# Limits through one partition, a list of places for all pieces of work, and bit operations placed one by one, in a fused attention and feed-forward kernel

## The chip, the cores and the metric

The kernel runs on one core of one Trainium2 chip. Its engines work side by side, each through its own queue in order: TensorE (PE, with its weight loads as PEld), VectorE (DVE), ScalarE (ACT), GpSimd (POOL) and SyncE (SP), which here issues nearly all DMA transfers. The metric is the device time of one execution in microseconds (us); less is better.

## The reference

Sliding-window attention with a few global keys, then a feed-forward layer with a piecewise-quadratic activation. Four batches, 8 heads, 768 positions, head size 64; the feed-forward layer sees 3072 rows of 512, with an inner width of 2048.

```python
def _attn_ref(q, k, v, n_global, n_local):
    scores = (1.0 / np.sqrt(D)) * np.matmul(q, k.transpose(0, 1, 3, 2))
    rel = pos[:, None] - pos[None, :]
    is_global = pos[None, :] < int(n_global)
    is_local = (rel >= 0) & (rel < int(n_local))
    keep = is_global | is_local
    dist = np.where(is_global & ~is_local, float(n_local), np.abs(rel))
    bias = -slopes[:, None, None] * dist[None, :, :]
    scores = np.where(keep, scores + bias[None], -1e9)
    a = softmax(scores)
    return np.matmul(a, v)

def _moe_ref(x, w_in, w_out):
    h = x @ w_in
    g = np.where(h >= 1, h, np.where(h <= -1, 0.0, (h + 1) ** 2 / 4.0))
    return g @ w_out
```

`n_global` (8) and `n_local` (96) are inputs, 64-bit integers in device memory. `w_in` and `w_out` come as 64-bit floats, so the kernel has to make 32-bit floats of them from their two halves with bit operations.

## The kernel before

**Tiles.** A unit is a block of 128 query rows of one batch; there are 24. The first four units are the first blocks of the four batches; they see one block of keys and run in 32-bit floats (`first_*`). The other 20 see their own block, the one before it and the global keys; they run with each operand split in two 16-bit halves (`put_unit` and what it calls). A unit is handled in two halves of four heads (`hf`). Two units make a chunk of 256 rows for the feed-forward layer; there are 12 chunks.

**Feed-forward.** `ffn1(c, g)` is 24 matmuls of 256 columns (2 blocks of 128 inner columns, 4 blocks of the depth, three products of halves) into one PSUM tile; `gelu(c, g, s)` follows in five steps (s = 0 on ScalarE, 1 and 2 on VectorE, 3 on ScalarE, 4 on GpSimd); `ffn2(c, t, f)` is three matmuls of 512 columns that add inner block `f` into the output of row tile `t`. `ffn2(c, t, f)` needs weight piece 16 + f, `ffn1(c, g)` the pieces 2g and 2g + 1.

**Weights.** Each of the 32 pieces (16 of `w_in`, then 16 of `w_out`) is loaded as 512 KB of raw words into one of three buffers (`w_load`, line 279, SP's queue), put together by three VectorE operations over 128 x 512 (`w_bits`, lines 293, 295 and 298, one after the other, the middle result in a PSUM tile of a pool with one buffer), rounded to the high half (`w_hi`, ScalarE), scaled in place (`w_scale`, line 306: two pieces of three on ScalarE, the third on GpSimd, by `WENG`), and subtracted to the low half (`w_lo`, GpSimd).

**The limits.** The two integers are fetched to all 128 partitions (line 103, ScalarE's DMA queue), made one float each in four small VectorE operations (lines 107 to 114), and used in `distances` (lines 245 to 247) to build the table of distances, which `slope` scales to a bias for each head. `masked` (line 373) adds the bias and takes the row's limit, `expo` is the exponential. `positions` (line 215) makes a row of column numbers by doubling, the partition numbers by a small matmul (line 225), and the unit matrix. `warm` (line 261) issues matmuls of zeros.

**Keys and values.** `fetch` loads a block into a ring of six buffers (shared by first loads and fetches), `conv_hi` and `conv_lo` make the halves, `conv_check` squares the block for a later check. `keep_glob` keeps the global keys of a batch and `set_glob` copies them into the block before the unit's own (keys by GpSimd, line 528, by `KGE`; values by VectorE, line 530). `scores`, `attend` are the matmuls; `turn_p`, `turn_x` are transposes by DMA.

**What sets the order.** Every call is put in a plan with a planned time (`at`), the plan is sorted by time, and the calls are made in that order; each engine's queue gets its instructions in this order and keeps it. The planned times are constants at the head of the file and are not times of the chip. Waits between engines come from the tiles that are read and written. The weights are read a second time later for a check of their range (`check_load`, `check_reduce`).

Of the kernel before, what the change touches and what calls it, by code (L numbers as in the profile page):

```python
# [17 lines left out]
P = 128  # L18
# [30 lines left out]
WENG = "aap"  # L49
# [6 lines left out]
KGE = "gpsimd"  # L56
# [7 lines left out]
FLOAD = [-2.88, 2.56, 12.5, 19.72]  # L64
VLOAD = [-0.57, 11.85, 18.46, 26.87]
FIRST = [8.37, 11.4, 14.3, 17.89, 30.69, 41.68, 52.21, 58.42]
WARM = [(1.0, 10)]
WLOAD = [0.8, 1.0, 8.0]
WA = 3
T0 = 27.51  # L70
GA = 5.33
GB = 5.56
TAB = -0.77
TBC = -2.29
RC = 42.99
WL = 10.75
E3 = [-19.46, -14.0, -6.46, -0.47, 3.78, 9.72, 16.26, 20.67]
PER = 47.0
SOFF = -14.3
FETCH = 16.6  # L80
CONV = 8.83
KG = 4.08
CHK = 7.36
VCONV = 10.53
VFETCH = 8.51
AVL = 15.92
GEL = [2.7, 3.48, 4.29, 5.77, 6.57]
# [9 lines left out]
def attention_then_moe(ctx, tc, q, k, v, n_global, n_local, w_in, w_out, out):  # L97
# [9 lines left out]
    nf = cpool.tile([P, 2, 2], F32, name="nf")  # L107
    nc.vector.tensor_copy(nf, nraw)
    neg = cpool.tile([P, 2, 2], F32, name="neg")
    nc.vector.tensor_single_scalar(neg, nf, 0.0, op=ALU.is_lt)  # L110
    nlow = cpool.tile([P, 2], F32, name="nlow")
    nc.vector.scalar_tensor_tensor(nlow, neg[:, :, 0], 4294967296.0, nf[:, :, 0], op0=ALU.mult, op1=ALU.add)
    nval = cpool.tile([P, 2], F32, name="nval")
    nc.vector.scalar_tensor_tensor(nval, nf[:, :, 1], 4294967296.0, nlow, op0=ALU.mult, op1=ALU.add)
# [9 lines left out]
    with ExitStack() as fast:  # L124
        fast_path(fast, tc, q, k, v, ng, nl, w_in, w_out, out, half, nm, sums, sq, su)
# [43 lines left out]
def fast_path(ctx, tc, q, k, v, ng, nl, w_in, w_out, out, half, nm, sums, sq, su):  # L169
    nc = tc.nc  # L170

# [36 lines left out]
    zeros = const.tile([P, DM], F16, name="zeros")  # L208
# [5 lines left out]

    def positions():
        nc.vector.memset(zeros, 0.0)
        nc.vector.memset(jrow[:, 0:1], 0.0)
        one = const.tile([P, 1], F32, name="one")
        nc.vector.memset(one, 1.0)
        n = 1  # L220
        while n < WIN:
            nc.vector.tensor_scalar(jrow[:, n : 2 * n], jrow[:, 0:n], float(n), None, op0=ALU.add)
            n *= 2
        pps = ps_h.tile([P, 1], F32, tag="h", name="pps")
        nc.tensor.matmul(pps, jrow[0:1, 0:P], one[0:1, :], start=True, stop=True)
        nc.vector.tensor_copy(prow[:, 0:1], pps)
        nc.vector.tensor_scalar(prow[:, 1:2], pps, float(P), None, op0=ALU.add)
        nc.vector.tensor_scalar(ident, jrow[:, 0:P], prow[:, 0:1], None, op0=ALU.is_equal)

    dists = {}  # L230

    def distances(own):
# [11 lines left out]
        nc.vector.tensor_copy(gap[:, 0:w], jrow[:, 0:w])  # L244
        nc.vector.tensor_scalar(cut, gap, ng, BIG, op0=ALU.is_ge, op1=ALU.mult)
# [13 lines left out]
    fill = []  # L259

    def warm(n):
        if not fill:
            fill.append(ps_o.tile([P, DM], F32, tag="o", name="fill"))
        for _ in range(n):
            nc.tensor.matmul(fill[0], zeros[:, 0:P], zeros, start=True, stop=True)
# [19 lines left out]
    def w_bits(n, s):  # L285
# [3 lines left out]
        if s == 0:  # L289
            wbits[n] = ps_b.tile([P, *hi.shape[1:]], I32, tag="b", name=f"w{num}_bits")  # L290
        t = wbits[n]
        if s == 0:
            nc.vector.tensor_scalar(t, rh, 0x07FFFFFF, 3, op0=ALU.bitwise_and, op1=ALU.logical_shift_left)  # L293
        elif s == 1:
# [5 lines left out]

    def w_hi(n):
        num, src, hi, lo = piece(n)
        nc.scalar.activation(hi, wf[n], AF.Copy, scale=SW)
# [88 lines left out]
    def norm(u, hf, scale):  # L392
        whole(u, hf)
        c = u * H + hf * 4
        r = xp.tile([P, 4], F32, tag="r", name=f"r{u}_{hf}")
        nc.vector.tensor_scalar(r, sums[:, c : c + 4], TINY, scale, op0=ALU.add, op1=ALU.mult)
        nc.vector.reciprocal(r, r)
        rs[u, hf] = r
# [30 lines left out]
    def scale_x(u, hf):  # L429
        x = xp.tile([P, 4, D], F32, tag="x", name=f"x{u}_{hf}")  # L430
# [26 lines left out]
    def put_first(u, hf, s):  # L457
# [5 lines left out]
        at(s + FO[3], norm, u, hf, 1.0 / SV)  # L463
# [150 lines left out]
    def put_unit(u, s0, s1):  # L614
# [26 lines left out]
        for hf, s in ((0, s0), (1, s1)):  # L641
# [8 lines left out]
            at(t + UO[5], norm, u, hf, SP_)  # L650
# [98 lines left out]
    at(0.5, distances, True)  # L749
    for h in range(H):  # L750
# [9 lines left out]
    TB = T0 + 8 * GA + TAB  # L760
    R1 = TB + 8 * GB + TBC
    R2 = R1 + RC
    tw = []
    for g in range(8):
        t = T0 + GA * g
        tw += [t - WL, t - WL + GA / 2]
        put_ffn1(0, g, t)
        if WA:
            at(t + 2.65, warm, WA)
    for g in range(8):  # L770
        t = TB + GB * g
# [12 lines left out]
    for c in range(2, NU // 2):  # L784
# [208 lines left out]
```

## Time and profile before

| what | us |
|---|---|
| median of three runs (lowest, highest) | 649.54 (649.40, 650.46) |
| the profiled execution's own time | 649.53 |
| its span, first to last instruction | 647.7 |
| TensorE busy | 613.5 |
| VectorE busy | 426.8 |
| ScalarE busy | 407.6 |
| GpSimd busy | 288.3 |

The mean granted clock of TensorE is 0.965 over the span. The page of the profile gives each engine's busy time, and 40 slices of the span with the busy share in tenths; its groups are instructions of one line, operation and tile, with count, busy time, mean length, and what ended the idle time before them. A timeline row has start, length, engine, line, operation, what is written and read, and in brackets the idle time ahead of it and its releaser.

### The profile page before, as it was taken

Reading aid. Unit: us, or ns where it says so; the run is one execution under the profiler, and the core shown is the slowest. Engines: PE = TensorE matmul, PEld = TensorE weight load, DVE = VectorE, ACT = ScalarE, POOL = GpSimd, SP = SyncE. Lnnn points to the kernel's source line nnn. Section 1 sums busy time; section 2 is a strip of 40 time slices with the busy share of each in tenths; the row PEclk is TensorE's granted clock in tenths of the full one; section 3 lists DMA queues with packets and bytes.
Section 4 is the critical chain, followed back from the end, with each engine's and each line's share of the span. In section 5 each row is a group of like instructions: output and inputs, shape, how many; then the busy total and the mean of one; then the engine's idle time right before and its main releaser. Section 6 shows DMA issues by size and latency. Waiting matters only on the chain.

```text
span 647.7 us, 14690 instructions
## 1 busy us (share of the span) xinstructions
PE 613.5 (95%) x5588; PEld 420.1 (65%) x5588; DVE 426.8 (66%) x1093; ACT 407.6 (63%) x1060; POOL 288.3 (45%) x292
## 2 busy tenths in 40 slices
PE   5688898899999999999999999999999999999995
PEld 3555665565786766766776676677667667666652
DVE  4699989976686655655767756666766766743351
ACT  2566667898876776666677667657767667532220
POOL 0056466985357345344454444445534534322210
PEclk8678899799999999999999999999999999999998
DMA  5465455729573453254466375394574463431141
GB/s 194 129 197 163 141 160 204 229 67 186 150 156 59 104 135 108 54 149 129 115 164 176 101 191 156 86 196 127 141 202 138 101 195 97 114 124 57 42 161 40
DMA packets 144367, 88.08 MB, mean 136 GB/s; under 512 B 108448, under 2 KB 124832, under 8 KB 144288
## 3 DMA queue, kind: packets, MB, share of 16 engines
q1 hardware_dynamic: 144000, 87.05, 49.4%
q8 instruction: 46, 0.75, 0.5%
q14 instruction: 33, 0.27, 0.1%
q10 hardware_dynamic: 288, 0.00, 0.0%
HBM read 54.53 MB, written 6.29 MB: 94 GB/s over the span
## 4 chain that ended last, share of the span: by engine, by line
PE 79%; DVE 13%; ACT 4%; issue 2%; DMA 1%; POOL 0%; DVEq 0%; ACTq 0%
PE o L715 36%; PE h L672 32%; PE s L545 4%; PE av L588 4%; DVE w_bits L295 2%; DVE w_f L298 2%; DVE w_bits L293 2%; PE av L424 1%; DVE h L690 1%; ACT z L385 1%; DVE u L695 1%; DMA nraw<-in_n_local_dram 1%; DVE z L373 1%; ACT u L685 1%; DVE x L431 1%
## 5 line engine op out<-in xcount | busy, mean ns | idle before, releaser
L672 PE MATMUL h<-xt,wih 128*128 128x256 f16 x1536 | 262.5, 276 | 1.3 <-DVE u L695 0.9
L672 PE MATMUL h<-xt,wil 128*128 128x256 f16 x768 | 212.0, 276 | 0.0
L703 POOL TENSOR_TENSOR gl<-u,gh 128x512 f16<-128x512 f32 x96 | 120.4, 1254 | 192.1 <-ACT gh L699 166.9
L672 PEld LDWEIGHTS <-wih 128*128 128x128 f16 x1536 | 149.7, 99 | 33.1 <-DVE u L695 1.7
L385 ACT ACTIVATE z<-z,nm 128x256 f32<-128x256 f32 (+1 forms) x192 | 92.1, 481 | 93.0 <-DVE nm L373 92.7
L715 PE MATMUL o<-wol,gh 128*128 128x512 f16 x384 | 146.5, 381 | 1.4 <-POOL wol L317 1.4
L715 PE MATMUL o<-woh,gh 128*128 128x512 f16 x384 | 146.8, 382 | 0.3 <-ACT ob L729 0.3
L715 PE MATMUL o<-woh,gl 128*128 128x512 f16 x384 | 146.3, 381 | 0.0
L373 DVE CUSTOM_DVE_ANT_0 z<-s,bias 128x256 f32<-128x256 f32 (+1 forms) x192 | 69.2, 394 | 87.4 <-PE s L545 82.2
L715 PEld LDWEIGHTS <-gh 128*128 128x128 f16 x768 | 71.5, 98 | 68.7 <-issue 1.6
L690 DVE SCALAR_TENSOR_TENSOR h<-h,u 128x512 f32<-128x512 f32 x96 | 66.7, 695 | 71.1 <-ACT u L685 69.9
L699 ACT ACTIVATE gh<-u 128x512 f16<-128x512 f32 x96 | 59.7, 621 | 41.0 <-DVE u L695 40.9
L672 PEld LDWEIGHTS <-wil 128*128 128x128 f16 x768 | 76.0, 99 | 10.1 <-issue 0.5
L685 ACT ACTIVATE u<-h,half 128x512 f32<-128x512 f32 x96 | 64.5, 672 | 25.0 <-PE h L672 24.8
L695 DVE SCALAR_TENSOR_TENSOR u<-u,h 128x512 f32<-128x512 f32 x96 | 65.8, 686 | 4.9
L715 PEld LDWEIGHTS <-gl 128*128 128x128 f16 x384 | 37.7, 98 | 47.7 <-issue 3.0
L563 DVE SCALAR_TENSOR_TENSOR ph<-z,ph 128x1024 f16<-128x1024 f32 x40 | 54.4, 1360 | 15.2 <-ACT ph L561 15.2
L341 DVE TENSOR_REDUCE sq<-c_raw 128x1 f32<-128x256 f32 x128 | 48.7, 410 | 3.9 <-DMA c_raw<-in_moe_w_out_dram 3.9
L500 POOL TENSOR_SCALAR kr<-kr 128x512 f32<-128x512 f32 x24 | 17.2, 717 | 66.0 <-ACT kh L485 65.7
L561 ACT ACTIVATE ph<-z 128x1024 f16<-128x1024 f32 x40 | 42.2, 1056 | 1.1
L545 PEld LDWEIGHTS <-qh 64*128 64x128 f16 x960 | 27.4, 95 | 18.7 <-issue 10.4
L588 PEld LDWEIGHTS <-pt 128*128 128x128 f16 x960 | 33.5, 98 | 8.7
(93 smaller groups left out, 690.1 us busy)
## 6 DMA issues: line engine op xcount, KB each, us to landing
w_raw<-in_moe_w_in_dram SPq DMA_DIRECT2D x16, 512.0 KB, 3.6
w_raw<-in_moe_w_out_dram SPq DMA_DIRECT2D x16, 512.0 KB, 3.5
c_raw<-in_moe_w_in_dram SPq DMA_DIRECT2D x32, 256.0 KB, 3.2
c_raw<-in_moe_w_out_dram SPq DMA_DIRECT2D x32, 256.0 KB, 3.0
kr<-in_k_dram SPq DMA_DIRECT2D x28, 256.0 KB, 4.4
vr<-in_v_dram SPq DMA_DIRECT2D x28, 256.0 KB, 3.2
qr<-in_q_dram SPq DMA_DIRECT2D x24, 256.0 KB, 4.6
out_dram<-ob SPq DMA_DIRECT2D x24, 256.0 KB, 3.3
```

The costliest lines, as they stand in the source:

```text
L373: nc.vector.tensor_tensor_reduce(out=p32[u, hf][:, hh, :], in0=pts[u, hf][hh // 2][:, hh % 2, 0:n], in1=bias[:, 4 * hf + hh, base : base + n],
L385: nc.scalar.activation(z, z, AF.Exp, bias=nm[:, c : c + 1], scale=-1.0, accum_out=sums[:, c : c + 1])
L545: nc.tensor.matmul(pair[r][:, j, e * P : (e + 1) * P], qf[rows, a, 2 * hf + j, :], kf[rows, c, 2 * hf + j, :], start=(n == 0), stop=(n == 2),)
L563: nc.vector.scalar_tensor_tensor(phs[u, hf][:, 1, :], zf, SP_, phs[u, hf][:, 0, :], op0=ALU.mult, op1=ALU.subtract)
L588: nc.tensor.matmul(av[:, hh, :], pt[:, a, hh, kt, :], vt[:, c, h * D : (h + 1) * D], start=(n == 0), stop=(n == 5),)
L672: nc.tensor.matmul(hp[:, e, :], w[:, dc, f], xt[:, hf, 2 * a + j, :], start=(n == 0), stop=(n == 3 * NDC - 1),)
L685: nc.scalar.activation(us[c, g], hs[c, g], AF.Relu, bias=half, scale=2.0 / (SV * SW), accum_out=su[:, col : col + 1])
L690: nc.vector.scalar_tensor_tensor(ws[c, g], hs[c, g], 4.0 / (SV * SW), us[c, g], op0=ALU.mult, op1=ALU.max)
L695: nc.vector.scalar_tensor_tensor(dst, us[c, g], 4.0, ws[c, g], op0=ALU.min, op1=ALU.mult)
L699: nc.scalar.activation(gh, ws[c, g], AF.Copy)
L703: (nc.gpsimd if GL == "p" else nc.vector).tensor_sub(gl, ws[c, g], gt[c, g][0])
L715: nc.tensor.matmul(po, a[:, cs], w[:, f, :], start=(f == 0 and n == 0), stop=(f == NFC - 1 and n == 2))
```

## The change

What it does:

- The limits are fetched to one partition. `limits` makes the floats there and spreads them over the partitions with one matmul of a row of ones, and a copy from PSUM. `distances` is cut in two: what needs the limits is now `clip`.
- `positions` makes the small matmul after 128 column numbers and doubles to 256 behind it. The zeros for `warm` are 128 wide and read four times over.
- The three bit operations of a weight piece are entries of the plan of their own. Odd pieces of `w_in` use a second PSUM tile (`spare(1)`) for the middle result. Likewise the two steps of `norm`.
- All scalings of weight pieces are on ScalarE (`WENG`); the copies of global keys into blocks are on VectorE (`KGE`).
- A form that puts a piece's sign on by another way (`signed`) is added but not chosen (`WS = "d"`).
- The plan's constants change, and the sorted plan is no longer followed as it stands: a list `PLACE` of 2659 numbers gives the order in which its entries are called.

```diff
-WENG = "aap"
+WENG = "a"
-KGE = "gpsimd"
+KGE = "vector"
...
-WARM = [(1.0, 10)]
+WARM = [(1.0, 8)]
...
-CK0 = 248.03
-CK1 = 624.26
+CK0 = 199.09
+CK1 = 573.64
...
+BO = [1.94, 2.51]
+WS = "d"
+RO = 0.18
...
+PLACE = [
+    5, 0, 1, 2, 11, 3, 6, 4, 7, 9, 12, 38, 68, 20, 8, 10, 13, 151, 14, 15, 16, 17, 18, 19, 21, 22, 25, 23, 24,
...
+]
...
-    nraw = cpool.tile([P, 2, 2], I32, name="nraw")
+    nraw = cpool.tile([1, 2, 2], I32, name="nraw")
     for i, n in enumerate((n_global, n_local)):
-        getattr(nc, NQ).dma_start(nraw[:, i, :], n.bitcast(I32).partition_broadcast(P))
+        getattr(nc, NQ).dma_start(nraw[:, i, :], n.bitcast(I32).partition_broadcast(1))
...
+    def limits():
+        nf = const.tile([1, 2, 2], F32, name="nf")
+        neg = const.tile([1, 2, 2], F32, name="neg")
+        low = const.tile([1, 2], F32, name="nlow")
+        nc.vector.tensor_copy(nf, nraw)
+        nc.vector.tensor_single_scalar(neg, nf, 0.0, op=ALU.is_lt)
+        nc.vector.scalar_tensor_tensor(low, neg[:, :, 0], 4294967296.0, nf[:, :, 0], op0=ALU.mult, op1=ALU.add)
+        nc.vector.scalar_tensor_tensor(low, nf[:, :, 1], 4294967296.0, low, op0=ALU.mult, op1=ALU.add)
+        nps = ps_h.tile([P, 2], F32, tag="h", name="pps_n")
+        nc.tensor.matmul(nps, ones[0:1, :], low, start=True, stop=True)
+        nc.vector.tensor_copy(nval, nps)
...
         if s == 0:
-            wbits[n] = ps_b.tile([P, *hi.shape[1:]], I32, tag="b", name=f"w{num}_bits")
+            if num < NFC and num % 2:
+                wbits[n] = spare(1).bitcast(I32).rearrange("p (a b) -> p a b", a=NDC)
+            else:
+                wbits[n] = ps_b.tile([P, *hi.shape[1:]], I32, tag="b", name=f"w{num}_bits")
...
-        at(t, lambda: [w_bits(n, s) for s in range(3)])
+        at(t, w_bits, n, 0)
...
+            at(t + BO[0], w_bits, n, 1)
+            at(t + BO[1], w_bits, n, 2)
...
-            at(t + UO[5], norm, u, hf, SP_)
+            at(t + UO[5], norm, u, hf, SP_, 0)
+            at(t + UO[5] + RO, norm, u, hf, SP_, 1)
...
     at(0.5, distances, True)
+    at(0.6, limits)
+    at(0.7, clip, True)
...
     with tc.manual_schedule():
-        for t, n, f, args in plan:
+        for n in PLACE or range(len(plan)):
+            t, _, f, args = plan[n]
```

More of the change, by code (lines that the diff above doesn't have):

```diff
@@ L124, in attention_then_moe @@
     with ExitStack() as fast:
-        fast_path(fast, tc, q, k, v, ng, nl, w_in, w_out, out, half, nm, sums, sq, su)
+        fast_path(fast, tc, q, k, v, nraw, nval, w_in, w_out, out, half, nm, sums, sq, su)
     good = cpool.tile([P, 2 * NU * H + NSQ + 2 * NFC + NSU + 3], F32, name="good")
@@ L166, in to_f32, with fast_path @@
     nc.vector.scalar_tensor_tensor(dst, lo, 29, t, op0=ALU.logical_shift_right, op1=ALU.bitwise_or)
-def fast_path(ctx, tc, q, k, v, ng, nl, w_in, w_out, out, half, nm, sums, sq, su):
+def fast_path(ctx, tc, q, k, v, nraw, nval, w_in, w_out, out, half, nm, sums, sq, su):
     nc = tc.nc
+    ng, nl = nval[:, 0:1], nval[:, 1:2]
     def pool(name, bufs, **kw):
@@ L224, in positions @@
         pps = ps_h.tile([P, 1], F32, tag="h", name="pps")
-        nc.tensor.matmul(pps, jrow[0:1, 0:P], one[0:1, :], start=True, stop=True)
+        nc.tensor.matmul(pps, jrow[0:1, 0:P], ones[0:1, 0:1], start=True, stop=True)
+        nc.vector.memset(zeros, 0.0)
+        nc.vector.tensor_scalar(jrow[:, P:WIN], jrow[:, 0:P], float(P), None, op0=ALU.add)
         nc.vector.tensor_copy(prow[:, 0:1], pps)
@@ L257, in slope, with spare @@
             nc.vector.tensor_scalar(bias[:, h, base : base + n], dists[own], c, None, op0=ALU.mult)
-    fill = []
+    spares = []
+    def spare(n):
+        if not spares:
+            spares.extend(ps_o.tile([P, DM], F32, tag="o", name=f"spare{e}") for e in range(2))
+        return spares[n]
     def warm(n):
-        if not fill:
-            fill.append(ps_o.tile([P, DM], F32, tag="o", name="fill"))
         for _ in range(n):
-            nc.tensor.matmul(fill[0], zeros[:, 0:P], zeros, start=True, stop=True)
+            nc.tensor.matmul(
+                spare(0).rearrange("p (a b) -> p a b", a=4), zeros, zeros.unsqueeze(1).to_broadcast([P, 4, P]),
+                start=True, stop=True,
+            )
     def piece(n):
@@ L299, in w_bits, with signed, w_sign @@
             wf[n] = f.bitcast(F32)
+    def signed(n):
+        return WS[n % len(WS)] == "s"
+    def w_sign(n):
+        nc.gpsimd.tensor_tensor(wf[n], wf[n], wraw[n][:, :, :, 1].bitcast(F32), op=ALU.mult)
+        did.add(("sign", n))
     def w_hi(n):
         num, src, hi, lo = piece(n)
+        after(("sign", n)) if signed(n) else None
         nc.scalar.activation(hi, wf[n], AF.Copy, scale=SW)
@@ L390, in whole, with norm @@
         after(*((("e", u, hf, hh)) for hh in range(4)))
-    def norm(u, hf, scale):
-        whole(u, hf)
+    def norm(u, hf, scale, s):
         c = u * H + hf * 4
[L395 to L398, printed above, removed]
+        if s == 0:
+            whole(u, hf)
+            rs[u, hf] = xp.tile([P, 4], F32, tag="r", name=f"r{u}_{hf}")
+            nc.vector.tensor_scalar(rs[u, hf], sums[:, c : c + 4], TINY, scale, op0=ALU.add, op1=ALU.mult)
+        else:
+            nc.vector.reciprocal(rs[u, hf], rs[u, hf])
+            did.add(("r", u, hf))
     tps = {}
@@ L429, in scale_x @@
     def scale_x(u, hf):
+        after(("r", u, hf))
         x = xp.tile([P, 4, D], F32, tag="x", name=f"x{u}_{hf}")
@@ L462, in put_first @@
         at(s + FO[2], first_turn, u, hf)
-        at(s + FO[3], norm, u, hf, 1.0 / SV)
+        at(s + FO[3], norm, u, hf, 1.0 / SV, 0)
+        at(s + FO[3] + RO, norm, u, hf, 1.0 / SV, 1)
         at(s + FO[4], first_pt, u, hf)
@@ L783, in fast_path @@
         put_unit(u, R1 + E3[2 * u - 2 * B], R1 + E3[2 * u - 2 * B + 1])
-    for c in range(2, NU // 2):
+    for c in range(2, NCH):
         t0 = R2 + PER * (c - 2)
```

125 lines of the change are left out of this document (71 added, 54 removed), and 138 rows, old and new, of the table PLACE.

## The prediction

> **What bounds the kernel now.** I read the stretches first (the view that gives each engine's busy time by window), then the chain of work that ended last, then TensorE's and VectorE's timelines. Columns of the first fence behind the page's first line: window, its length, busy time and count of PE, PEld, DVE, ACT, POOL, the granted clock, DMA share, GB/s.
>
> ```profile
> span 647.7 us, 14690 instructions
> ...
> 11.66:36.20 24.54, 17.78 (x87) 13.96 (x88) 15.45 (x61) 13.41 (x46) 4.09 (x4) 0.57 0.43 141
> 36.20:130.90 94.70, 80.75 (x566) 55.31 (x566) 87.72 (x185) 66.03 (x163) 60.21 (x59) 0.89 0.56 178
> 129.80:640.70 510.90, 509.58 (x4921) 348.62 (x4920) 318.90 (x814) 326.59 (x854) 224.83 (x226) 1.00 0.49 126
> ...
> 129.80:176.00 46.20, 44.99 (x478) 28.11 (x477) 31.83 (x85) 40.38 (x111) 27.38 (x29) 1.00 0.58 133
> ```
>
> From 129.80 to 640.70 TensorE is busy 509.6 of 510.9 us at full clock: nothing there can be won but by doing less, and the change removes no matmul from it. Whatever time is won is won before 130 us. There VectorE is the full engine, 87.7 of 94.7 us between 36.2 and 130.9, while between 11.66 and 36.20 it idles 9.1 us of 24.5.
>
> What fills VectorE is the weights. Each of 32 pieces needs three bit operations, and in the timeline one piece starts 2.17 us after the other (36.21, 38.38), so 0.72 us per operation and 69 us for all:
>
> ```profile
> L295 DVE SCALAR_TENSOR_TENSOR w_bits<-w_raw,w_bits 128x512 int32<-128x512 int32 x32 | 22.3, 696 | 1.1
> L298 DVE SCALAR_TENSOR_TENSOR w_f<-w_raw,w_bits 128x512 int32<-128x512 int32 x32 | 22.0, 688 | 2.9
> ...
> 23.47 0.69 DVE L293 TENSOR_SCALAR w_bits<-w_raw 128x512 int32<-128x512 int32 x1
> 36.21 0.68 DVE L293 TENSOR_SCALAR w_bits<-w_raw 128x512 int32<-128x512 int32 x1
> 38.38 0.69 DVE L293 TENSOR_SCALAR w_bits<-w_raw 128x512 int32<-128x512 int32 x1
> 94.89 0.69 DVE L298 SCALAR_TENSOR_TENSOR w_f<-w_raw,w_bits 128x512 int32<-128x512 int32 x1
> 97.50 1.16 POOL L317 TENSOR_TENSOR wol<-w_f,woh 128x512 f16<-128x512 f32 x1 [1.57 <-ACT w_f L310]
> 130.18 0.69 DVE L298 SCALAR_TENSOR_TENSOR w_f<-w_raw,w_bits 128x512 int32<-128x512 int32 x1
> ```
>
> The first piece begins at 23.47, the last ends at 130.87. From a piece's last bit operation to its low half on GpSimd it is 3.1 us (95.58 to 98.66). So a floor can be drawn: end of TensorE = (end of the bits of a piece) + 3.1 + (TensorE work left in the order when that piece is first used). Work is counted with the spans of a full-clock stage of the chain, 2.62 us for an ffn1 step (24 matmuls), 2.59 for four ffn2 steps (12), and 0.8 for a scores or attend:
>
> ```profile
> 612.66 2.62 PE h L672 x24
> 615.28 2.59 PE o L715 x12
> ```
>
> At 129.80 step ffn1(1,5) has ended, 509.6 us of work is left; 8.1 us of it (scores, attend, ffn1, six ffn2) lie ahead of the first use of piece 31. Its floor is 130.87 + 3.1 + 501.5 = 635.5. TensorE ended at 640.7, 5.2 later, and the reason is in its timeline: it waited for unit 4's queries, and came back at half clock (nine ffn2 matmuls 0.43 apart where 0.22 is usual, 1.9 us). 3.2 + 1.9 = 5.1.
>
> ```profile
> 116.23 1.25 PE L545 MATMUL s<-kh,qh 64*128 64x128 f16 x20 [3.19 <-POOL qh L501]
> 117.81 0.63 PE L715 MATMUL o<-wol,gh 128*128 128x512 f16 x1
> 118.24 0.63 PE L715 MATMUL o<-woh,gl 128*128 128x512 f16 x1
> ```
>
> **The change part by part.** The order is fixed by the list: sorting the new plan by planned time and reading the list gives every engine's queue. Planned times themselves set nothing any more.
>
> *The start.* All of the attention needs the two limits. Before:
>
> ```profile
> 2.67 0.58 PE L225 MATMUL pps<-one,bias 1*128 1x1 f32 x2 [2.67 <-DVE bias L222]
> 3.19 4.45 PE L265 MATMUL fill<-zeros 128*128 128x512 f16 x10
> 7.31 0.17 DVE L108 CAST nf<-nraw 128x4 f32<-128x4 int32 x1 [4.69 <-DMA nraw<-in_n_local_dram]
> 9.47 0.29 DVE L245 TENSOR_SCALAR m<-m,nval 128x128 f32<-128x128 f32 x1
> 10.57 1.18 DVE L257 TENSOR_SCALAR bias<-m 128x128 f32<-128x128 f32 x8
> 11.66 0.28 DVE L373 CUSTOM_DVE_ANT_0 z<-s,bias 128x128 f32<-128x128 f32 x1
> ...
> q10 hardware_dynamic: 288, 0.00, 0.2%
> nraw<-in_n_local_dram ACTq DMA_DIRECT2D x1, 1.0 KB, 6.1
> w_raw<-in_moe_w_in_dram SPq DMA_DIRECT2D x14, 512.0 KB, 3.6
> ```
>
> The fetch to 128 partitions is 288 tiny packets and lands 6.1 us after its issue. Two single rows are not in the trace: between the 6.1 of this row and nothing. I take under 4.5, since a 512 KB load lands in 3.6. Then the matmul that spreads them stands behind eight warming matmuls on TensorE: 3.19 + 8 x 0.44 = 6.7, + 0.58 as the other small float matmul, + 0.17 for a copy as small as the cast, + 2.19 for clip and slopes (9.47 to 11.66, as before): first masked head at 9.6 instead of 11.66. With the old landing three more small steps on VectorE (0.5) come behind 7.31, then the same 2.9: 10.9. Gain 0.8 to 2.1, taken 2.1.
>
> *Weights early, bits singly.* The new order starts piece 0 behind the eighth masked head and strews single bit operations between the attention steps, where before 9.1 us were idle. I follow the first two units through it with these durations (TensorE at the low clock, as there):
>
> ```profile
> 18.42 1.23 PE L362 MATMUL s<-kr,qr 64*128 64x128 f32 x8
> 21.15 1.94 PE L424 MATMUL av<-vr,pt 128*128 128x64 f32 x8 [1.50 <-DVE xt L455]
> 22.89 1.06 PE L406 MATMUL tp<-ident,z 128*128 128x128 f32 x4
> 23.74 0.64 PE L445 MATMUL xtp<-ident,x 128*128 128x128 f32 x2
> 34.44 0.63 PE L672 MATMUL h<-xt,wih 128*128 128x256 f16 x2
> ```
>
> VectorE still waits six times for scores, products or transposes: 0.7, 0.8, 0.7, 0.4, 0.9, 1.6, together 5.1 us, until the first ffn1 step can run, at about 38.5 (before 34.44, but with three pieces of bits done and four half-units scored; now six and seven). So 9.1 - 5.1 = 4.0 us of idle are gone. A load needs a free raw buffer, that is the bits three pieces back; by the order 5 to 6 us of VectorE work lie between, more than the 3.6 of the row, so loads are covered while SP's queue moves. Up to piece 31 the queue holds the same work as before, but three value splits and two small copies come ahead of it and two gelu steps go behind: +1.5. Last bits: 9.6 + (130.87 - 11.66) + 1.5 - 4.0 = 126.3, that is 4.6 earlier. Behind 36 us I leave VectorE as full as before.
>
> *A new order at the end of the weights.* ffn2 of pieces 28 and 29 now stands ahead of ffn1(1,5), so piece 29 decides: it ends 8 us ahead of piece 31 (between them six bit operations, 4.3, two gelu steps, 1.4, one split, 1.4, and two heads of twice the columns of the 0.28 above), at 118.3.
>
> ```profile
> L695 DVE SCALAR_TENSOR_TENSOR u<-u,h 128x512 f32<-128x512 f32 x17 | 11.6, 681 | 0.6
> L563 DVE SCALAR_TENSOR_TENSOR ph<-z,ph 128x1024 f16<-128x1024 f32 x8 | 11.5, 1434 | 2.2 <-ACT ph L561 2.2
> ```
>
>  Work left there: 509.6 - 2.6 + 2.6 + 1.3 = 510.9. Floor 118.3 + 3.1 + 510.9 = 632.3; by piece 31 it is 126.3 + 3.1 + 501.5 = 630.9. The larger holds.
>
> *The wait for unit 4.* Its k and q conversions move from TensorE's 66th us of work to its 49th, with scores(4,0) at the 71st in both; the 3.19 wait goes. Something will be late in its place; I add 1.7, a third of the old 5.1 (both ends, 0 and 5.1, stay in the range). TensorE ends at 632.3 + 1.7 = 634.0, **6.7 us** before the old 640.7; what follows (last copy, store, 7.0 us) is unchanged. Against the profiled 649.53 us, which is the median shown to 0.01, that is 642.8.
>
> *Moved between engines.*
>
> ```profile
> L312 POOL TENSOR_SCALAR w_f<-w_f 128x512 f32<-128x512 f32 x10 | 6.2, 618 | 4.3 <-ACT wih L303 2.9 <-ACT woh L303 1.1
> L528 POOL COPY kh<-kg 128x256 f16<-128x256 f16 x4 | 2.8, 706 | 1.9 <-PE s L545 1.9
> ...
> 57.54 1.15 POOL L703 TENSOR_TENSOR gl<-u,gh 128x512 f16<-128x512 f32 x1
> 58.19 0.54 DVE L396 TENSOR_SCALAR r<-sums 128x4 f32<-128x4 f32 x1
> ```
>
> Ten scalings go from GpSimd to ScalarE, 6.2 us; ScalarE is busy 66 of 94.7 there, so nothing, and a piece's path keeps its 3.1. If that cover is gone it costs 0.6 a piece on pieces it delays. Sixteen copies of keys go to VectorE, about 0.7 each as on GpSimd, one before piece 31, fifteen under a full TensorE. The weight checks begin earlier, all under 1.00 clock with VectorE at 62%: nothing. Splitting norm and the second bits buffer add no work; 32 warming matmuls replace 34.
> The Trainium skill, "SBUF — State Buffer", section "SBUF: two separate sides", speaks against the copies: a GpSimd operation holds the port pair it shares with VectorE to its end, and a fast VectorE copy then stands still. The trace agrees (the four-column operation at 58.19 ends at 58.73, when GpSimd's of 57.54 does, at 58.69), and by that rule a copy would cost up to 1.2 more, once on the path.
>
> **Rivals.**
> *The clock comes early.* With more matmuls between 10 and 36 us, TensorE may run at full clock there. A product step is then 1.10 instead of 1.94:
>
> ```profile
> 72.72 1.10 PE L424 MATMUL av<-vr,pt 128*128 128x64 f32 x8
> ```
>
> Then the six waits, 5.1, all but vanish: 637.7. For: 17.8 of 24.5 us busy already. Against: 0.57 in just this stretch, with waits in every half-unit, which the new order keeps. The Trainium skill, "TensorE: Matmul & The Clock Gate", section "Part 1: The HAM clock gate", has full rate after some 3.4 us of sustained activity, which would give this case; the 0.57 in a stretch that is mostly busy speaks against it.
> *A wait takes the place of the old one.* Units 4 to 7 now have to be ready about 7 us sooner, with ScalarE already busy 40.4 of 46.2 us between 129.8 and 176 and nothing taken from it there. If TensorE waits there for a transpose as it did for the queries, it loses the whole 5.1 rather than 1.7: 646.2; with two such, 649 to 650, no change.
> *Slower: SP's queue.* Before, unit 4's values were fetched behind the last weight load. Now they stand ahead of load 22, and need the buffer that the last first-unit product, av(3,1), reads. SP is in order:
>
> ```profile
> SPq L354 <- PE s L362: 7.7, 1, 7.7
> ```
>
> It stood so for 7.7 us before, at a first load that waited for TensorE. By the same count as above av(3,1) ends at 82 and piece 22 is wanted on VectorE at 91; with two more issues and 3.6 to land, the cover is 4 us. Beyond it each us late is lost to VectorE, the weights and TensorE alike, and it makes the kernel slower from 4 + 6.7 = 10.7 us late. The fetches of units 5 to 7, which stand among loads 20 to 31 and wait for ScalarE's checks, can do the same: two waits of 7.7 beyond the cover give 642.8 + 15.4 = 658.2. For: TensorE is the late one at these products, and the stall feeds itself, since TensorE then waits for the weights. Against: before, no weight load is named among what VectorE waited for.
> *The list changes nothing at the start* (loads land late, piece 0 still at 20): gain only of the vanished 5.1 less 1.7: 646.1.
>
> **How the numbers follow.** Forecast, 639.5 to 645.5 around 642.8: 0.57. Early clock, 635 to 639.5: 0.13. A wait in place or the start unchanged, 645.5 to 648.2: 0.15. No change within 0.2% (1.3 us, about what a measurement here can tell): 0.05. Slower: 0.10. Faster is 0.57 + 0.13 + 0.15 = 0.85. Range 636.5 to 648.5: it leaves out half of the early clock's lower part and the slower case.
>
> **What would show it.** First masked head at 9.6 to 10.9; first bits before 14; VectorE's idle between the first head and 36 us near 5; last bits at 126; no wait for qh ahead of scores(4,0); TensorE without waits behind 130 and its last matmul at 634. Wrong if VectorE waits for w_raw, if the last bits come after 129, or if TensorE idles more than 3 us between 110 and 175.

## The result, and the profile after

| | median us (lowest to highest, executions) | ratio to the kernel before, 95% interval |
|---|---|---|
| before | 649.73 (649.40 to 650.46, 4) | |
| changed | 639.76 (637.52 to 640.59, 4) | 0.9835 (0.9819 to 0.9851) |
| changed, once more in a later round | 640.01 (637.58 to 640.68, 5) | 0.9822 (0.9804 to 0.9841) |

The change makes the kernel about 10 us faster; the forecast was 642.8, with 636.5 to 648.5 as its range. The profiled execution of the changed kernel was the fastest of its four, 637.52 us with a span of 635.7. The later round's profile is of an execution of 640.45 us, nearer the median; where the two differ, both are given.

The stretches of the changed kernel's fastest execution first (window, length, busy time and count of PE, PEld, DVE, ACT, POOL, granted clock, DMA share, GB/s):

```profile
11.66:36.20 24.54, 22.18 (x129) 16.06 (x130) 22.52 (x88) 20.23 (x69) 6.94 (x6) 0.75 0.60 194
36.20:116.70 80.50, 70.11 (x545) 50.56 (x544) 78.29 (x151) 67.72 (x156) 53.71 (x50) 0.94 0.67 203
116.70:629.10 512.40, 507.38 (x4894) 346.36 (x4888) 334.52 (x825) 319.96 (x836) 235.86 (x206) 1.00 0.52 123
```

VectorE's idle time in the early window has shrunk from 9.1 us to 2.0 (24.54 less 22.52). The stage in which VectorE is full now ends at 116.7 instead of 130.9. Behind it TensorE is busy 507.4 of 512.4 us: 5.0 us idle, where the same part of the kernel before lost 1.3. VectorE's own timeline shows where the 14 us come from:

```profile
4.21 0.15 DVE L380 CAST nf<-nraw 1x4 f32<-1x4 int32 x1
6.98 0.16 DVE L386 COPY nval<-pps_n 128x2 f32<-128x2 f32 x1 [2.06 <-PE pps_n L385]
9.41 0.28 DVE L566 CUSTOM_DVE_ANT_0 z<-s,bias 128x128 f32<-128x128 f32 x1
...
12.36 0.69 DVE L468 TENSOR_SCALAR w_bits<-w_raw 128x512 int32<-128x512 int32 x1
...
72.75 0.69 DVE L468 TENSOR_SCALAR w_bits<-w_raw 128x512 int32<-128x512 int32 x1
73.48 0.69 DVE L472 SCALAR_TENSOR_TENSOR w_bits<-w_raw,w_bits 128x512 int32<-128x512 int32 x1
74.28 0.69 DVE L475 SCALAR_TENSOR_TENSOR w_f<-w_raw,w_bits 128x512 int32<-128x512 int32 x1
75.00 0.69 DVE L468 TENSOR_SCALAR w_bits<-w_raw 128x512 int32<-128x512 int32 x1
75.60 0.69 DVE L888 SCALAR_TENSOR_TENSOR h<-h,u 128x512 f32<-128x512 f32 x1
...
108.14 0.68 DVE L475 SCALAR_TENSOR_TENSOR w_f<-w_raw,w_bits 128x512 int32<-128x512 int32 x1
115.98 0.68 DVE L475 SCALAR_TENSOR_TENSOR w_f<-w_raw,w_bits 128x512 int32<-128x512 int32 x1
```

The first masked head is at 9.41, the first bits at 12.36, the last bits end at 116.66. Read the four rows from 72.75 by their **starts**. Every one is 0.69 long. But L472, which reads what L468 wrote, begins 0.73 behind it, L475 0.80 behind L472, and the next L468, which overwrites the same PSUM tile, 0.72 behind L475. The gelu step at 75.60, which needs nothing of the operation ahead, begins 0.60 behind it. An operation's length in the profile doesn't say what it holds VectorE for; the distance to the next start does. In the kernel before, the three operations of a piece stand together, and mostly the first of the next piece behind them:

```profile
120.56 0.69 DVE L293 TENSOR_SCALAR w_bits<-w_raw 128x512 int32<-128x512 int32 x1
121.29 0.70 DVE L295 SCALAR_TENSOR_TENSOR w_bits<-w_raw,w_bits 128x512 int32<-128x512 int32 x1
122.09 0.69 DVE L298 SCALAR_TENSOR_TENSOR w_f<-w_raw,w_bits 128x512 int32<-128x512 int32 x1
122.82 0.69 DVE L293 TENSOR_SCALAR w_bits<-w_raw 128x512 int32<-128x512 int32 x1
```

From such distances, added up row by row (less the named wait ahead of the next row), VectorE's time from the first head to the start of the last bits divides so:

| us | first head to last bits | 95 bit operations | named waits | all else |
|---|---|---|---|---|
| before | 118.5 | 68.5 (0.72 each) | 10.6 | 39.4 |
| changed (637.52) | 106.6 | 60.6 (0.64 each) | 3.4 | 42.6 |
| changed (640.45) | 109.2 | 60.9 | 5.1 | 43.2 |

So the bits cost 7.9 us less and the waits 7.2 less, and 3.2 us more of all else (gaps that no row names among it) lies ahead of the last piece. TensorE's timeline in the changed kernel (what it waited for in brackets) shows what this is worth at the end:

```profile
72.26 1.09 PE L601 MATMUL tp<-ident,z 128*128 128x128 f32 x4 [3.87 <-DVE u L893]
109.41 0.38 PE L913 MATMUL o<-wol,gh 128*128 128x512 f16 x1 [0.41 <-POOL wol L502]
112.20 0.38 PE L913 MATMUL o<-wol,gh 128*128 128x512 f16 x1 [1.33 <-POOL wol L502]
119.31 0.38 PE L870 MATMUL h<-xt,wih 128*128 128x256 f16 x2 [0.26 <-DVE u L893]
...
629.08 0.38 PE L913 MATMUL o<-woh,gl 128*128 128x512 f16 x1
```

The wait that ends at 112.20 is for the low half of piece 29, whose bits ended at 108.82. From there to the start of the last matmul are 516.9 us. In the execution of 640.45 us the two rows of piece 29 (VectorE's, then TensorE's) lie 2.7 us later:

```profile
110.82 0.69 DVE L475 SCALAR_TENSOR_TENSOR w_f<-w_raw,w_bits 128x512 int32<-128x512 int32 x1
114.88 0.38 PE L913 MATMUL o<-wol,gh 128*128 128x512 f16 x1 [1.33 <-POOL wol L502]
```

The wait for unit 4's queries is gone. Among its waits a new kind has come, seen in the list of waits (total, times, longest):

```profile
PE av L785 <- DMA pt<-ph: 4.3, 5, 1.4
```

`attend` waits five times for the DMA transposes of P, between 229 and 522 us, where before TensorE stood full.

### The profile page after: what moved, and what is told of

Its sections match the earlier page's. It is cut to its first block, busy times and chain, and to the rows that moved or that the text cites. A ratio compares the mean times of both kernels' runs of the same rounds, so it can differ in the third digit from the quotient of the medians.

```text
span 635.7 us, 14747 instructions
## 1 busy us (share of the span) xinstructions
PE 607.6 (96%) x5588; PEld 417.1 (66%) x5588; DVE 442.2 (70%) x1109; ACT 412.1 (65%) x1070; POOL 296.8 (47%) x266
## 4 chain that ended last, share of the span: by engine, by line
issue 31%; POOL 26%; PE 25%; DVE 9%; ACT 5%; DMA 2%; POOLq 0%; SPq 0%; ACTq 0%; DVEq 0%
PE o L913 13%; POOL gl L901 11%; PE h L870 8%; POOL xh L801 8%; POOL kh L698 2%; POOL kr L697 2%; DVE w_f L475 2%; POOL qh L698 2%; ACT z L578 1%; POOL qr L697 1%; DMA w_raw<-in_moe_w_out_dram 1%; PE av L785 1%; POOL wol L502 1%; DVE u L893 1%; PE s L742 1%
## 5 line engine op out<-in xcount | busy, mean ns | idle before, releaser
L870 PE MATMUL h<-xt,wih 128*128 128x256 f16 x1536 | 259.7, 274 | 0.7 <-DVE u L893 0.7
L901 POOL TENSOR_TENSOR gl<-u,gh 128x512 f16<-128x512 f32 x96 | 117.8, 1227 | 214.2 <-ACT gh L897 205.2
L566 DVE CUSTOM_DVE_ANT_0 z<-s,bias 128x256 f32<-128x256 f32 (+1 forms) x192 | 67.1, 397 | 22.2 <-PE s L742 20.4
L760 DVE SCALAR_TENSOR_TENSOR ph<-z,ph 128x1024 f16<-128x1024 f32 x40 | 61.6, 1540 | 9.6 <-ACT ph L758 9.4
L801 POOL TENSOR_TENSOR xh<-x,xh 128x256 f16<-128x256 f32 x40 | 62.2, 1554 | 10.4 <-ACT xh L799 8.8
L785 PE MATMUL av<-vh,pt 128*128 128x64 f16 x960 | 34.6, 193 | 4.5 <-DMA pt<-ph 4.3
## 6 DMA issues: line engine op xcount, KB each, us to landing
w_raw<-in_moe_w_in_dram SPq DMA_DIRECT2D x16, 512.0 KB, 4.0
w_raw<-in_moe_w_out_dram SPq DMA_DIRECT2D x16, 512.0 KB, 3.8
```

Of the source, the lines that this page charges most:

```text
L566: nc.vector.tensor_tensor_reduce(out=p32[u, hf][:, hh, :], in0=pts[u, hf][hh // 2][:, hh % 2, 0:n], in1=bias[:, 4 * hf + hh, base : base + n],
L760: nc.vector.scalar_tensor_tensor(phs[u, hf][:, 1, :], zf, SP_, phs[u, hf][:, 0, :], op0=ALU.mult, op1=ALU.subtract)
L785: nc.tensor.matmul(av[:, hh, :], pt[:, a, hh, kt, :], vt[:, c, h * D : (h + 1) * D], start=(n == 0), stop=(n == 5),)
L801: (nc.gpsimd if XL == "p" else nc.vector).tensor_sub(xhs[u, hf][:, 1, :], xs[u, hf], xhs[u, hf][:, 0, :])
L870: nc.tensor.matmul(hp[:, e, :], w[:, dc, f], xt[:, hf, 2 * a + j, :], start=(n == 0), stop=(n == 3 * NDC - 1),)
L901: (nc.gpsimd if GL == "p" else nc.vector).tensor_sub(gl, ws[c, g], gt[c, g][0])
```

## The experiments

Two questions: is it the single placing of the bit operations that pays, and where; and what sets the end now? All twelve were timed against the kernel before.

**The bits of a piece together again.** Right behind the sorting of the plan, the first two operations of each piece are moved in the list to stand ahead of the third. (`order` is a copy of the list, here and below, and `spot` gives an entry's number.)

```diff
+    for n in range(2 * NFC):
+        for s in (1, 0):
+            m = spot["w_bits", n, s]
+            order.remove(m)
+            order.insert(order.index(spot["w_bits", n, s + 1]), m)
```

> The changed kernel with one edit: in its list the first two bit operations of every piece stand directly ahead of the third, so that each depends on the one just ahead of it. Theory A (an operation that needs the result of the one just ahead of it holds VectorE longer): some 50 more neighbours of one piece, each 0.72 to 0.79 us from start to start where 0.60 is seen with another operation between them, make 6 to 7 us more of VectorE before the last piece; last bits at 122 to 124 instead of 116.7, time 642 to 646 us. Theory B (only the filled idle time of the start counted): last bits within 1 us of 116.7, time 637.5 to 640.6 us like the changed kernel.

Measured: 652.05 us, ratio to before 1.0030 (1.0018 to 1.0042): all of the gain is gone. The last bits end at 129.38. In VectorE's timeline the second operation of a piece starts 0.71 to 0.73 behind the first, and the third 0.80 behind the second in most pieces (0.73 in seven):

```profile
113.50 0.69 DVE L468 TENSOR_SCALAR w_bits<-w_raw 128x512 int32<-128x512 int32 x1
114.22 0.70 DVE L472 SCALAR_TENSOR_TENSOR w_bits<-w_raw,w_bits 128x512 int32<-128x512 int32 x1
115.02 0.69 DVE L475 SCALAR_TENSOR_TENSOR w_f<-w_raw,w_bits 128x512 int32<-128x512 int32 x1
```

Divided as above: bits 67.3, named waits 9.7, all else 42.8. Theory A holds for the bits (6.4 to 6.7 us more than in the two profiles of the changed kernel), but missed the other half: the waits rise by 4.6 to 6.3 us too, so that the last bits and the time came later than it said. My reading of the waits, which no run isolates: a block of 2.2 us on VectorE holds up a masked head or a gelu step behind it, then TensorE and ScalarE, and in the end VectorE itself.

**The same for the pieces 7 to 31 alone**, those behind 36 us (`range(7, 2 * NFC)` in the edit above).

> The changed kernel with the first two bit operations of a piece directly ahead of the third for the pieces 7 to 31 alone; pieces 0 to 6, which fill the idle time of the first 36 us, stay as the change has them. Theory A (most of the gain of placing them singly lies behind 36 us, where VectorE is full, as 50 shorter operations and fewer waits): last bits at 126 to 129, time 647 to 651 us. Theory B (the filled start carries it, and single placing behind it only shortens operations by some 5 us): last bits at 120 to 123, time 641 to 645 us.

Measured: 647.95 us, ratio 0.9957 (0.9943 to 0.9970), last bits at 126.17, bits 66.4, waits 7.9. Theory A, at its lower edge. Against the 640.01 of the changed kernel in the same round this is 7.9 us; with the first seven pieces also grouped it was 12.0 (652.05 less 640.01, from two rounds). So about two thirds of what single placing brings arises where VectorE was full already, and one third where it fills the early idle time.

**Single placing in the kernel before**, with nothing else of the change.

```diff
-        at(t, lambda: [w_bits(n, s) for s in range(3)])
+        for s in range(3):
+            at(t + 0.9 * (s - 1), w_bits, n, s)
```

> The kernel before with one edit: the three bit operations of a piece are planned 0.9 us apart around the old place instead of as one block; by its order 54 of 95 neighbours of bit operations remain. Theory A (single placing alone shortens VectorE): about 41 operations go from 0.72 to 0.79 us to 0.60, 5 to 6 us, and some of the 10.6 us of named waits go too; last bits 5 to 10 us earlier than 130.9, time 641 to 646 us. Theory B (TensorE was held by the wait for unit 4's queries and not by the weights alone, so without the new order behind it nothing is won): last bits earlier, time 648 to 651 us.

Measured: 649.50 us, ratio 0.9981 (0.9970 to 0.9991). The time is B's, but not for B's reason: the last bits end at 132.05, no earlier at all. Bits fell to 65.7 us while the named waits rose to 14.4. Even offsets break up only some neighbours: 54 of the 95 bit operations still have behind them one that reads or overwrites their result, against 73 in the kernel before and 22 in the changed one. With these offsets, the only ones tried, single placing alone wins no time; that it needs a list that puts the right steps between is my reading.

The bits follow this count from run to run. For 22 such neighbours they take 60.6 us, for 39 (the run without the list, below) 63.8, for 54 (this run) 65.7, for 55 (pieces 7 to 31 grouped) 66.4, for 67 (all grouped) 67.3, for 73 (before) 68.5: about 0.15 us for each.

**The list taken out**, so that the planned times set the order (`PLACE = []`).

> The changed kernel with its list taken out: the work is issued in the order of the planned times, in which a step stands 30 places away from its place in the list on average. Theory A (the order written out is what keeps bit operations apart and TensorE fed): bit operations again 0.65 to 0.70 us each and more named waits on VectorE, low half of piece 29 at 118 to 124 us instead of 112 to 115, time 644 to 650 us. Theory B (the planned times already give the gain and the list only repeats them): time within 2 us of 640.0.

Measured: 692.64 us, ratio 1.0647 (1.0628 to 1.0665), far beyond both theories. TensorE's longest waits in it:

```profile
PE av L645 <- DMA pt<-ph: 21.9, 15, 6.9
PE tp L461 <- ACT z L438: 14.9, 11, 2.8
```

The bits are as theory A had them (63.8 us, 0.67 each), but VectorE's named waits up to the last bits are 28.6 us, and the last bits end at 136.72, 17.4 behind the 119.33 of the execution of 640.45 us. From there to the last matmul, which starts at 682.87, are 546.2 us instead of 512.5. So two thirds of the loss lie behind the weights, in good part in waits for P like the first row. The new constants are no plan that stands by itself; the order written out is worth 52.6 us on top of them.

**The limits fetched to 128 partitions again**, worked out there, no matmul.

```diff
-    nraw = cpool.tile([1, 2, 2], I32, name="nraw")
+    nraw = cpool.tile([P, 2, 2], I32, name="nraw")
...
-        nc.vector.scalar_tensor_tensor(low, nf[:, :, 1], 4294967296.0, low, op0=ALU.mult, op1=ALU.add)
-        nps = ps_h.tile([P, 2], F32, tag="h", name="pps_n")
-        nc.tensor.matmul(nps, ones[0:1, :], low, start=True, stop=True)
-        nc.vector.tensor_copy(nval, nps)
+        nc.vector.scalar_tensor_tensor(nval, nf[:, :, 1], 4294967296.0, low, op0=ALU.mult, op1=ALU.add)
```

> The changed kernel with the two limits fetched to all 128 partitions again and worked out there, without the small matmul. Theory A (VectorE is full from the first head on, so the start is on the path): cast at 7.3 instead of 4.2, first masked head at 10.5 to 11.5 instead of 9.41, last bits later by as much, time 1.0 to 2.0 us over that of the changed kernel, 639 to 642 us. Theory B (the start is made up for by slack between VectorE and TensorE): last bits later, time within 0.5 us of the changed kernel.

Measured: 639.28 us, ratio 0.9834 (0.9821 to 0.9847), no different from the changed kernel. VectorE's timeline has the late landing and a first head 0.9 us later than 9.41:

```profile
7.27 0.17 DVE L380 CAST nf<-nraw 128x4 f32<-128x4 int32 x1 [2.98 <-DMA nraw<-in_n_local_dram]
10.31 0.28 DVE L563 CUSTOM_DVE_ANT_0 z<-s,bias 128x128 f32<-128x128 f32 x1
```

Theory B: the low half of piece 29 comes at 114.84, against 114.88 in the changed kernel's execution of 640.45 us. Of the 2.25 us by which the first head moved (11.66 to 9.41) only 0.9 are the one-partition fetch and its matmul, and they buy nothing that these measurements show.

**Sixteen key copies back on GpSimd, and ten scalings back on GpSimd**, each alone (`KGE = "gpsimd"`; `WENG = "aap"`).

> The changed kernel with the sixteen copies of global keys back on GpSimd. Theory A (the copies on VectorE, up to 1.4 us where GpSimd holds the port, delay the low halves of P and so the transposes that attend waits for): the waits for P fall below 2 us in sum, time 2 to 3 us under the changed kernel. Theory B (the copies are hidden on either engine, and the waits come from the order of the transposes): the waits stay at 3.5 to 4.5 us, time within 1 us of the changed kernel.

> The changed kernel with ten of the 32 weight scalings back on GpSimd. Theory A (ScalarE was too full for them, 38 of 43 us busy between 82 and 125, so a piece's path from bits to low half grew from 3.1 to 3.4 us): the low half of piece 29 comes up to 0.3 us earlier, time 0.3 to 1 us under the changed kernel. Theory B (ScalarE covers them as the prediction had it): time within 1 us of the changed kernel's 640.0, either way.

Measured: 638.55 us, ratio 0.9804 (0.9787 to 0.9822), and 637.54 us, ratio 0.9805 (0.9784 to 0.9826). Both overlap the changed kernel's 0.9822 (0.9804 to 0.9841): neither move shows a gain, and whether either costs 1 to 2 us stays open. The mechanisms that theory A named are not there: the waits for P are still 3.9 us without the copies, and piece 29 takes 3.4 us from the end of its bits to the wait's end with the scalings on either engine.

**The window bias later**: `distances`, `clip` and the slopes of the later units 46 places on in the list, out of the way of the gelu step behind the wait of 3.87 us.

```diff
+    late = [n for n in order if plan[n][2].__name__ in ("distances", "clip", "slope") and plan[n][3][0] is False]
+    for n in reversed(late):
+        m = order.index(n)
+        order.insert(m + 46, order.pop(m))
```

> The changed kernel with the distances, the clip and the eight slopes of the window bias 46 places later in its list, behind the last transposes of the first units. Theory A (the wait of 3.87 us ahead of those transposes at 72.3 us comes from this block on VectorE, and TensorE is ahead of no other limit there): the wait falls below 1 us, time 2 to 4 us under the changed kernel, 634 to 637.5 us. Theory B (VectorE is full, so what is won at 72 us is waited for a few steps later): TensorE's waits between 72 and 125 us keep their sum of about 6 us, time within 1 us of the changed kernel.

Measured: 640.07 us, ratio 0.9854 (0.9840 to 0.9868). TensorE's timeline shows the wait move on rather than go:

```profile
68.65 0.63 PE L601 MATMUL tp<-ident,z 128*128 128x128 f32 x4 [0.65 <-DVE u L893]
79.39 0.38 PE L870 MATMUL h<-xt,wih 128*128 128x256 f16 x2 [2.62 <-DVE u L893]
...
114.55 0.38 PE L913 MATMUL o<-wol,gh 128*128 128x512 f16 x1 [1.34 <-POOL wol L502]
```

Theory B. TensorE is not what decides there: it stands before piece 29 again, with the same last wait.

**The transposes of P first.** For the units from 10 on, the copy of global values goes behind the low half of P on VectorE, and `turn_p` ahead of the `turn_x` of the unit before on SyncE's queue.

```diff
+    def move(what, behind):
+        a, b = order.index(spot[what]), order.index(spot[behind])
+        if a < b:
+            order.insert(b, order.pop(a))
+
+    for u in range(8, NU):
+        for hf in range(2):
+            if UNITS[u][1] >= 2:
+                move(("set_glob", u, "v"), ("split_p", u, 0, 1))
+            move(("turn_x", u - 1 + hf, 1 - hf), ("turn_p", u, hf))
```

> The changed kernel with two moves in its list for the units from 10 on: the copy of the global values stands behind the low half of P on VectorE instead of ahead of it, and the transpose of P stands ahead of the transpose of X on SyncE's queue. Theory A (the five waits of attend for the transposes of P, 4.3 us in sum, come from this order): P lands 2 to 2.5 us earlier, the waits vanish, time 3 to 4.5 us under the changed kernel, 633.5 to 636.5 us, and the executions lie closer together. Theory B (the landing itself is slow, 4.3 to 6.2 us, and the transposes hold each other up in the DMA engines): the waits stay above 3 us in sum, time 637.5 to 640.6 us.

Measured: **633.43 us, ratio 0.9748 (0.9736 to 0.9761)**, the fastest version of all. In the changed kernel the copy (first row), 1.41 us long, stands ahead of the low half, and the transpose of X takes SyncE for 1.20 ahead of that of P:

```profile
364.92 1.41 DVE L727 COPY vh<-vg 32x1024 f16<-32x1024 f16 x1
366.25 1.21 DVE L760 SCALAR_TENSOR_TENSOR ph<-z,ph 128x1024 f16<-128x1024 f32 x1
...
368.69 1.20 SPq L809 DMA_TRANSPOSE xt<-xh  x1
369.99 1.95 SPq L767 DMA_TRANSPOSE pt<-ph  x1
...
374.31 0.87 PE L785 MATMUL av<-vh,pt 128*128 128x64 f16 x24 [0.48 <-DMA pt<-ph]
```

With the order turned round no wait for P is left, and the last matmul starts 512.0 us behind the wait for piece 29 instead of 516.9. These 4.9 us are what the trace accounts for. Up to 218 us both versions run the same instructions in the same order, so that piece 29 comes 2.3 us earlier in this profile (109.94 against 112.20) is not the edit's doing; the profile is of its fastest execution, 630.61 us. The medians differ by 6.6, and the 1.7 beyond the 4.9 are not explained. The transposes themselves still take 4.3 us from issue to landing, so theory B is out: the order was at fault. Two things were moved at once, the copy and the transposes, and which of them counts is not shown. That the executions would lie closer together, as theory A had it, did not come: 630.61 to 634.45.

**Two steps moved behind piece 29**, on top of that version: the split of unit 5's values with its check, and a copy of global values.

```diff
+    for what in (("conv_check", 5, "v", 2), ("conv_lo", 5, "v", 2), ("keep_glob", 4, "v")):
+        move(what, ("w_bits", 29, 2))
```

> The version with the transposes of P first, and besides the split of unit 5's values (with its check) and the copy of unit 4's global values moved behind the last bit operation of piece 29 on VectorE. Theory A (TensorE ends 516.9 us, here 512.0, after the low half of piece 29, so VectorE work moved behind that piece is won in full): low half 1.5 to 2 us earlier, time 631 to 632.5 us. Theory B (the two steps were hidden or hold back a buffer that the weight loads need): time 633 to 635 us.

Measured: 635.95 us, ratio 0.9782 (0.9763 to 0.9801), above both theories and slower than the version it builds on (633.43, in another round; the intervals just miss each other). Nothing shows a gain on VectorE: from the end of piece 20's bits to the end of piece 29's it is 27.8 us, against 27.7 in the version it builds on; two new waits of 0.3 us each have come into this stretch. And the moved check now stands ahead of the piece's high half on ScalarE, and waits there for the moved split; TensorE waits twice. ScalarE's timeline, then TensorE's:

```profile
110.63 0.63 ACT L706 ACTIVATE vr<-vr 128x512 f32<-128x512 f32 x1 [1.62 <-DVE vh L692]
...
111.92 0.62 ACT L488 ACTIVATE woh<-w_f 128x512 f16<-128x512 f32 x1
```

```profile
112.59 0.38 PE L913 MATMUL o<-woh,gh 128*128 128x512 f16 x1 [1.58 <-ACT woh L488]
114.48 0.38 PE L913 MATMUL o<-wol,gh 128*128 128x512 f16 x1 [1.52 <-POOL wol L502]
```

From bits to the end of the wait for the low half are 4.8 us instead of 3.4. So 1.4 us were lost on ScalarE, through a step that I moved without asking what was behind it.

**And the ffn2 steps of pieces 28 and 29 behind ffn1(1,5)** on TensorE, besides.

```diff
+    for f, x in ((13, 1), (13, 0), (12, 1), (12, 0)):
+        move(("ffn2", 0, x, f), ("ffn1", 1, 5))
```

> As the version with the two steps moved, and besides the four ffn2 steps of pieces 28 and 29 behind ffn1(1,5) on TensorE. Theory A (the waits of 0.42 and 1.34 us for these pieces go, and piece 31 becomes the floor about 3 us below): time another 1 to 1.8 us lower, 629.5 to 631 us. Theory B (the next pieces or the gelu steps are then waited for): the waits appear at pieces 30 or 31 or at ffn1, time within 0.6 us of the version without it.

Measured: 639.03 us, ratio 0.9815 (0.9797 to 0.9833), 3 us worse again. The wait is where theory B put it, at ffn1, but costs far more than the 0.6 us that it allowed. ffn1(1,5) needs the PSUM tile that a gelu step frees, and this step starts at 113.69 on VectorE, behind the moved steps, a split of P and two of piece 30's bit operations:

```profile
114.41 0.59 PE L870 MATMUL h<-xt,wih 128*128 128x256 f16 x2 [4.80 <-DVE u L893]
```

**The changed kernel again** gave the second line of the table at the head.

> The changed kernel itself once more beside the others, for the spread of its executions: 637.5 to 641 us, ratio to before 0.982 to 0.986; if the spread comes from the first 120 us, the last bits lie 1 to 3 us later than the 116.7 of the profiled execution that was the fastest, while the five waits for P again come to 4 to 5 us.

It came as expected: piece 29's low half at 114.88 instead of 112.20, the last bits ending at 119.33, then the same 516.9 us and 4.4 us of waits for P. The whole difference between the two executions is there before 100 us. Across the variants that keep the list, without the two last moves, the end follows one rule, whatever the edit:

| us | wait for piece 29 ends | last matmul starts | between |
|---|---|---|---|
| changed (637.52) | 112.20 | 629.08 | 516.9 |
| changed (640.45) | 114.88 | 631.83 | 516.9 |
| limits to 128 partitions | 114.84 | 631.51 | 516.7 |
| scalings on GpSimd | 112.60 | 628.11 | 515.5 |
| key copies on GpSimd | 114.33 | 630.61 | 516.3 |
| window bias later | 114.55 | 630.81 | 516.3 |
| pieces 7 to 31 grouped | 121.30 | 638.28 | 517.0 |
| all pieces grouped | 124.50 | 641.62 | 517.1 |
| transposes of P first | 109.94 | 621.94 | 512.0 |

## Why the prediction came out as it did

**What bounds the kernel** was right: nothing is won behind 130 us, all of it ahead, through VectorE and the weights. **Piece 29 decides** was right as well: in every row of the table TensorE waits for its low half. The sum itself went off in two terms, on opposite sides, and by 1.6 to 1.7 us in the work left, of which 0.7 are small waits.

| term | predicted | measured (637.52 / 640.45) |
|---|---|---|
| bits of piece 29 end | 118.3 | 108.8 / 111.5 |
| from there to the low half | 3.1 | 3.4 / 3.4 |
| TensorE's work left there | 510.9 | 516.9 less the waits for P: 512.6 / 512.5 (small waits, 0.7 us, in it) |
| waits behind it | 1.7 | 4.3 / 4.4 for P |
| last matmul starts | 634.0 | 629.1 / 631.8 |

**The term that was mis-sized** is "Behind 36 us I leave VectorE as full as before", with "0.72 us per operation" for all 96. I took 0.72 from the kernel before, where 73 of 95 bit operations have behind them one that reads or overwrites their result, and carried it over to an order that leaves 22 of them. Pulled apart, the same operation holds VectorE for 0.60, and 7.9 us are gone from the bits alone. The grouping experiments show it from the other side: 5.5 to 6.7 us of bits come back when the operations stand together. The early idle time was mis-sized too, the smaller part: 5.1 us of waits were expected up to 36 us, 2.0 to 2.6 (24.54 less 21.94) were left. Last bits: predicted at 126.3, measured at 116.7 and 119.3. Of these 9.6 us in the profile of 637.52 us, the bits are 7.9, the waits 3.2 (7.2 gone where 4.0 were counted) and the first head 0.2, and 1.7 go the other way (3.2 more of all else where 1.5 were counted).

**What I added for new waits** came true in kind and not in place. "Something will be late in its place" had TensorE in mind near unit 4. Nothing is late there; the new waits stand where I had counted TensorE as full, in the steady part, and are 4.3 instead of 1.7 us. They and the work left hid a good part of what VectorE had won, so that 642.8 came out only 3 us above the median. That the number fell so near is in part luck: piece 29 was off by 9.5 and 6.8 us, and some 2.6 of new waits and 1.7 of work took part of it back.

**The start.** Predicted first head 9.6, measured 9.41 and 9.50; landing, warming matmuls and the small matmul each within 0.4 us of the working (cast at 4.21, copy of the limits at 6.98). But taking its 2.1 us at full value was wrong. Without the small matmul the head is 0.9 later and the time the same.

**Moved between engines: nothing.** Not refuted, and not settled within 2 us, see above. The Trainium skill's rule on the port pair of VectorE and GpSimd ("SBUF — State Buffer", "SBUF: two separate sides"), weighed in the prediction at up to 1.2 us once on the path, is borne out by the rows of the changed kernel. A key copy without a GpSimd operation beside it takes 0.22; the one ahead of piece 31's last bits takes 1.06, and ends 0.09 behind the GpSimd operation that had begun before it:

```profile
114.81 1.16 POOL L901 TENSOR_TENSOR gl<-u,gh 128x512 f16<-128x512 f32 x1
115.00 1.06 DVE L725 COPY kh<-kg 128x256 f16<-128x256 f16 x1
...
328.01 0.22 DVE L725 COPY kh<-kg 128x256 f16<-128x256 f16 x1
...
364.90 1.15 POOL L901 TENSOR_TENSOR gl<-u,gh 128x512 f16<-128x512 f32 x1 [5.18 <-ACT gh L897]
364.92 1.41 DVE L727 COPY vh<-vg 32x1024 f16<-32x1024 f16 x1
...
536.55 0.40 DVE L727 COPY vh<-vg 32x1024 f16<-32x1024 f16 x1
```

The copy of values ahead of the low half of P is held in the same way: 1.41 us behind a GpSimd operation, 0.40 where none had begun before it. In the time no run shows it for the key copies: the one on VectorE's way to piece 31 stands behind the bits of piece 29 (108.82), which decide, and the ratios with the copies on either engine overlap.

**The rivals.** *The clock comes early* did not come: the granted clock up to 36 us was 0.75 and 0.67. The waits nearly vanished all the same. The window of the later execution:

```profile
11.66:36.20 24.54, 22.69 (x123) 16.72 (x123) 21.94 (x87) 20.02 (x68) 6.94 (x6) 0.67 0.60 195
```

TensorE is busy 22.7 of 24.5 us in it. By the rule that the prediction drew from the Trainium skill ("TensorE: Matmul & The Clock Gate", "Part 1: The HAM clock gate"), full rate after some 3.4 us of sustained activity, it should have been near 1; the trace disagrees, as far as the busy share can stand for sustained activity. In the version with the limits on 128 partitions, TensorE was busy 22.1 us of the same window, and the clock was 0.93. *A wait takes the place of the old one* is half true: 4.3 us, but by way of SyncE's order and not of ScalarE. *Slower by SP's queue* did not happen: no weight load is among what VectorE waited for. *The list changes nothing at the start* is out, with the first bits at 12.36.

## What to carry to other kernels

On a full VectorE, count an operation by the distance to the next start, not by its length, and look at whether the next one needs its result: interleaving independent work took 7.9 us off the same 96 operations here. When a late stage is rigid, find the one wait behind which everything keeps its distance; only what moves that wait, or a wait behind it, moves the time. Before a step is moved, look at what stands behind its new place on every engine that it uses.

## What was not expected of the hardware

A 128x512 bit operation of 0.69 us holds VectorE 0.59 to 0.61 us in nearly all cases when the next one is independent, 0.72 when the next reads its result from a tensor_scalar, and up to 0.80 between the two scalar_tensor_tensor steps. A next operation that only **overwrites** the tile just read also pays: in the changed kernel L468 starts 0.70 to 0.73 behind L475 when both use the same PSUM tile (9 cases) and 0.58 to 0.61 when it writes another (5 cases). The Trainium skill ("VectorE: DVE Perf Modes", "The DRAIN you can't avoid") has the next operation start only when the pipe is empty, at the same cost with or without semaphores, but adds that one which is not held starts earlier; its rules for kernel authors advise to minimize the count of operations. The trace agrees with the exception, and with the count unchanged the order matters: the independent neighbour starts 0.09 us before the profile's end of the operation ahead, the dependent one 0.03 to 0.11 behind it. Also not expected: the same instructions in the same order take 2.7 us more or less up to 100 us from one execution to the next (piece 29 at 112.20 and 114.88). The granted clock differs there, 0.75 against 0.67 up to 36 us, but the version with the limits on 128 partitions had 0.93 in that window and was no earlier, so the cause is open.
